# Sliding-window attention and MLP on one core: fill products on 64 rows, maxima of four heads at once, values by query block, division after the values

## Chip, cores and metric

The kernel runs on one core of a Trainium2 chip. The metric is the device time of one execution in microseconds (us). Lines of the profile name engines: PE is TensorE's products, PEld its weight loads, DVE is VectorE, ACT is ScalarE, POOL is GpSimd, SP is the queue that issues all DMA transfers of this kernel.

## What is computed

```python
def _A_ref(x, wqkv, wo):                    # x [1, 2048, 512], 32 heads of 16, window 256
    q, k, v = split_of(x @ wqkv)
    scores = einsum("bhqd,bhkd->bhqk", q, k) * 16 ** -0.5
    mask = (i - j >= 0) & (i - j < 256)
    p = softmax(where(mask, scores, -1e9))
    return einsum("bhqk,bhkd->bhqd", p, v).reshape(B, S, D) @ wo
def _B_ref(x, w1, b1, w2, b2):              # 1792 features
    return gelu(layernorm(x) @ w1 + b1) @ w2 + b2
xn = layernorm(x)
out = x + _A_ref(xn) * silu(_B_ref(xn))
```

## The kernel before

**Precision.** A product in full precision is three products of operands cut into a high and a low part (`PASSES`, L70: high·high, high·low, low·high). `split` (L72) makes the parts: a cast on ScalarE for the high one, a subtraction on VectorE for the low one.

**Operands.** The normalised x is kept transposed in `big` (high and low, 4 contraction tiles of 128, 2048 tokens). The 32 heads are worked on in 8 quads n of four heads. `job_qk` (L235) makes the query and key rows of quad n for a chunk c of 512 tokens: 12 products of 128 rows by 512 columns into one bank of PSUM, tile `pj`; its `finish` copies the bank to `pjr` (ScalarE), casts to `sh` (`high`, L257) and subtracts to `sl` (`low`, L264, GpSimd), and six DMAs (`send`, L248; four of `sh`, two of `sl`) lay the rows out in `slots[n % 2]`, tile `qk`. There a head has a strip of rows holding the high and low parts with which one 64-row product gives the scores in full precision; four rows hold the (negated) row maxima for the exponential. Each head of a pair p has its own half, rows 0 to 63 or 64 to 127, so the two products of a pair use different halves of TensorE. Tiles `sh` and `sl` are in pool `sgp`, which has one buffer of each.

**Slots.** The loop at L591 runs over slots t from -16 to 128. Slot t holds block t of the *probabilities* (quad t // 16, key block t % 16) and, `LEAD` = 12 blocks ahead, block m = t + 12 of the *maxima*. The order of one slot is written out:

```python
prob_block(t, pair 1); max_block(m, pair 0); fill_in(t, 0)
max_block(m, pair 1); prob_block(t, pair 0); fill_in(t, 1)
pv_step(t - 1); max_rows(m) if m % 4 == 3; plan[t]; out_rows
```

`Ordered` (L32) issues every instruction, so all lines of the profile are L42; it keeps the order of the program on every engine but SP, whose order a scheduler sets.

- `max_block` (L303): two score products of up to 384 keys into a two-bank tile `mx` (two such buffers), one predicated copy that writes the first key block over the masked part of the last one, and one reduction of 512 elements to two heads' maxima `mt`.
- `max_rows` (L323): negates the maxima of four blocks, cuts them into two parts, transposes them, and lays them out in the `qk` rows through a DRAM tile `mT_d`, by two DMAs.
- `prob_block` (L340): two score products, transposed, with 384 queries into a bank each (`st`, two buffers), an exponential of each on ScalarE (for the last 12 slots one exponential of both banks, into the free `mx` banks), and two maskings on GpSimd (`affine_select`). Result `pt`, 7 buffers.
- `pv_step` (L395): for key block kb, four heads' products into `otb`, one bank that collects 512 queries; the 17th value column is one, so the sum of the probabilities comes out beside the values. Every fourth block `out_chunk` (L378) transposes `otb` (VectorE), takes the reciprocal of the sums and multiplies (GpSimd), and `out_rows` (L389) transposes back and stores to `oT_d`.
- *Fills* are TensorE's other work, put between the products of a slot: in slots -16 to -1 quad 0's operands, all values of the first 16 heads (`job_v`, L273) and the transposes of x (`job_x`); from then on `job_qk` of quads 1 to 7, `job_v` of the other 16 heads (slots 49 to 77), and from slot 106 the transposes of y (`job_y`) and the first MLP products of six feature tiles (`job_h`, L464), which are kept in DRAM until the MLP. `level` (L533) spreads a job's products over its slots such that each slot holds TensorE about as long. `later` (L227) puts `high` one half slot and `low` three half slots behind a job's last product; the jobs of the four chunks of a quad follow each other at about four slots.
- `plan` holds other steps by slot: loading and splitting weights, the layernorm of y.

**MLP.** The loop over four chunks c at the end makes `hidden(f)` (12 products of 128x512 into `h`), `activate` (gelu, cast, subtraction) and `project` (12 products into four banks `acc`) for 14 feature tiles, software-pipelined by two; at f = 10 to 13 `load_o` (L642) loads and splits the attention values of 128 tokens each. At the end of a chunk come the products with `wo` (`s`, 12 of 512 columns for each block of 128 tokens), the gate, and the store.

Of the kernel before, what the change touches and what calls it, by code (L numbers as in the profile page):

```python
# [31 lines left out]
class Ordered:  # L32
    """an engine whose instructions keep the order of the program."""
# [16 lines left out]
def mixer_kernel(ctx, tc, x, wqk, wv, wo, w1, b1, w2, b2, out):  # L50
    """x [S,D]; wqk [NQ,128,KT*128]; wv [2,128,KT*256]; wo [128,4*512];
    w1 [128,NF*KT*128]; b1 [128,NF]; w2 [128,NF*512]; b2 [512]; out [S,D]."""
# [7 lines left out]
    ps_mx = ctx.enter_context(tc.tile_pool(name="ps_mx", bufs=2, space=PSUM))  # L60
    ps_st = ctx.enter_context(tc.tile_pool(name="ps_st", bufs=2, space=PSUM))
    ps_ot = ctx.enter_context(tc.tile_pool(name="ps_ot", bufs=1, space=PSUM))
    ps_pj = ctx.enter_context(tc.tile_pool(name="ps_pj", bufs=1, space=PSUM))
    attn = ExitStack()
    vp = attn.enter_context(tc.tile_pool(name="vp", bufs=1))
    pp = attn.enter_context(tc.tile_pool(name="pp", bufs=7))
    o2p = attn.enter_context(tc.tile_pool(name="o2p", bufs=1))
# [68 lines left out]
    XE, XO = ((pp, "pt"),), tuple((o2p, f"o2_{i}") for i in range(4))  # L136
    XA = (XE, XO, XE[:1] * 3 + ((t2, "t2"),), XO)

# [1 line left out]
    xs = {0: load_x(0, XA[0], "x")}  # L140
    big = bigp.tile([P, 2, KT, S], F32R, tag="big", name="xnT")       # x normalised, transposed; hi, lo
    x3 = bigp.tile([P, 4, 512], F32, tag="qk1", name="x_3")
    slots = []                                          # row, q/k, pair, token
# [7 lines left out]
    xn_d = dram.tile([4, P, D], F32, name="xn_d")      # the first chunk normalised  # L151
    oT_d = dram.tile([4, P, S], F32, name="oT_d")
    h_d = dram.tile([EARLY, P, 512], F32, name="h_d")          # the mlp's first products made early
    mT_d = dram.tile([NQ, NCH, 32, P], F32, name="mT_d")       # minus the row maxima, by rows
    otb = ps_ot.tile([P, 512], F32, name="otb")
# [13 lines left out]
    mask = upper.bitcast(I32).unsqueeze(1).to_broadcast([P, 2, P])  # L169
    neg = negc.unsqueeze(2).to_broadcast([P, 2, P])  # L170
    b1s = const.tile([P, NF], F32, name="b1s")

# [1 line left out]
    def job_x(c):  # L174
        box = []

        def mm(k):
            kt, i = k // 4, k % 4
            if i == 0:
                if kt == 2:  # L180
                    box.append(otb)
                elif kt == 3 and c == 0:
                    box.append(ps_mx.tile([P, 2, 512], F32, tag="mx", name="tr_0_3")[:, 0])
                else:
                    box.append((ps_st if kt < 2 else ps_pj).tile([P, 512], F32, tag="b", name=f"tr_{c}_{kt}"))
# [16 lines left out]
    def halves(dst_hi, dst_lo, src, part):  # L202
        """split in two steps, on ScalarE and on VectorE; part None: both."""
# [23 lines left out]
    def later(k, fn):  # L227
        """fn at k half slots from now."""
# [6 lines left out]
    def job_qk(n, c):  # L235
        """query and key rows of quad n, chunk c."""
# [4 lines left out]
        def mm(i):  # L241
            if i == 0:
                box.append(ps_pj.tile([P, 512], F32, tag="b", name=f"pj_{n}_{c}"))
# [29 lines left out]
    def job_v(hf, i):  # L273
        """value rows of token blocks 2i and 2i+1, 16 heads."""
        box = []

        def mm(k):
            if k == 0:
                box.append((ps_pj if hf else ps_st).tile([P, 2, 256], F32, tag="b", name=f"pv_{hf}_{i}"))
# [8 lines left out]

    def spread(jobs, places):
        """the jobs' products over the places, in order, each job in places of its own."""  # L290
# [10 lines left out]
    mts = {}  # L301

    def max_block(n, qb, p):  # L303
        slot = slots[n % 2]
        if qb % 4 == 0 and p == 0:
            mts[n, qb // 4] = small.tile([P, 2, 2, 4], F32, tag="mt", name=f"mt_{n}_{qb}")
        ps = ps_mx.tile([P, 2, 512], F32, tag="mx", name=f"mx_{n}_{qb}_{p}")
        lo = max(qb - 2, 0)
        off = 384 - P * (qb + 1 - lo)
        for a in range(2):  # L310
            r = slice(64 * a, 64 * a + 64)
            nc.tensor.matmul(ps[:, a, off:384], slot[r, 0, p, P * qb: P * (qb + 1)],
                             slot[r, 1, p, P * lo: P * (qb + 1)], start=True, stop=True)
        if qb < 2:
            nc.vector.copy_predicated(ps[:, :, 256:384], mask, neg)
            off = 256 - P * qb
        else:
            nc.vector.copy_predicated(ps[:, :, 256:384], mask, ps[:, :, 0:128])
            off = 128
        nc.vector.tensor_reduce(out=mts[n, qb // 4][:, :, p, qb % 4],  # L320
                                in_=ps[:, :, off:384], axis=AX.X, op=ALU.max)

    def max_rows(n, c):  # L323
        """minus the maxima, in two parts, as rows of the queries' operand."""
        mt = mts.pop((n, c))
        mh = small.tile([P, 2, 2, 2, 4], F32R, tag="mh", name=f"mh_{n}_{c}")     # head, part, pair, block
        nc.vector.tensor_scalar(mh[:, :, 0], mt, -1.0, None, op0=ALU.mult)
        nc.vector.scalar_tensor_tensor(mh[:, :, 1], mt, -1.0, mh[:, :, 0].bitcast(F32),
                                       op0=ALU.mult, op1=ALU.subtract)
# [8 lines left out]
    pts = {}  # L338

    def prob_block(n, kb, p):  # L340
# [3 lines left out]
        wide = 16 * n + kb + LEAD >= 16 * NQ       # no maxima are left: their banks are free  # L344
        if wide:
            both = ps_mx.tile([P, 2, 512], F32, tag="mx", name=f"st_{n}_{kb}_{p}")
        for a in range(2):
            r = slice(64 * a, 64 * a + 64)
            ps = both[:, a] if wide else ps_st.tile([P, 512], F32, tag="b", name=f"st_{n}_{kb}_{p}_{a}")
            nc.tensor.matmul(ps[:, 0:w], slot[r, 1, p, P * kb: P * (kb + 1)],  # L350
                             slot[r, 0, p, P * kb: P * kb + w], start=True, stop=True)
            if not wide:
                nc.scalar.activation(pt[:, a, 0:w], ps[:, 0:w], AF.Exp, scale=DH ** -0.5)
        if wide:
            nc.scalar.activation(pt[:, :, 0:w], both[:, :, 0:w], AF.Exp, scale=DH ** -0.5)
# [9 lines left out]
    def pv(n, c, kb, first, last):  # L365
        """what key block kb adds to query chunk c."""
        q0 = max(P * kb, 512 * c)
        q1 = min(P * kb + 384, 512 * (c + 1))
        for j in range(4):
            h = (4 * n + j) % 16  # L370
            nc.tensor.matmul(otb[32 * j: 32 * j + DH + 1, q0 - 512 * c: q1 - 512 * c], vt[:, kb, h],
                             pts[(n, kb, j // 2)][:, j % 2, q0 - P * kb: q1 - P * kb],
                             start=first, stop=last, skip_group_check=True,
                             tile_position=(0, 32 * j))

    o2 = {}

    def out_chunk(n, c):  # L378
        g, half = n // 2, n % 2
        T = t2.tile([P, 16, 32], F32, tag="t2", name=f"T_{n}_{c}")  # L380
        nc.vector.transpose(T.rearrange("p b r -> p (b r)"), otb)
# [384 lines left out]
```

## Time and profile before

| what | value |
|---|---|
| time, median of 3 runs (lowest to highest) | 826.49 us (825.32 to 826.92) |
| span of the profiled execution, first to last instruction | 826.1 us |
| mean clock granted to TensorE | 0.994 |
| DMA bytes | 70.77 MB, mean 86 GB/s |
| exponential of 128x384 / of 128x768, ScalarE | 489 ns (x408) / 814 ns (x20) |
| predicated copy of 128x256, VectorE | 421 ns (x224) |
| reduction of 128x512, VectorE | 693 ns (x240) |
| transposes of values `T` / `oT`, VectorE | 715 ns (x32) / 702 ns (x16) |
| copy `pjr` / cast `sh`, ScalarE | 587 ns / 621 ns (x32 each) |
| first slot with probabilities starts at / last maxima at | 76.5 us / 444.9 us |
| MLP from | 481.7 us |

The profile comes from one execution; what lies around its span shows in the table as the difference to the runs' times. "Busy" is the time in which an engine has an instruction under way. A group line gives line, engine, operation, tiles written and read, shapes, count, then busy time and mean duration, then the idle time ahead of the group and what ended it. The chain that ended last is followed back from the last instruction, at each step to what released it.

### The profile page before, as it was taken

The numbers are of one execution on the slowest core, as the hardware profiler recorded it, in microseconds if no ns is written. First come the engines' busy times: TensorE is split into PE (matmuls) and PEld (weight loads), VectorE is DVE, ScalarE is ACT, GpSimd is POOL, SyncE is SP. The second block draws the span as 40 slices with busy tenths as digits, with TensorE's granted clock in tenths as the row PEclk, the third lists the DMA queues.
The fourth block names the chain that finished last, engine by engine and source line by source line (L and its number), as shares of the span: only waits on it lengthen the run. The fifth ranks groups of instructions, "written<-read, shape, count | busy, mean of one in ns | idle before, by whom it ended". The sixth has DMA issues, their size and how long they took to land.

```text
span 826.1 us, 13927 instructions
## 1 busy us (share of the span) xinstructions
PE 804.7 (97%) x4864; PEld 533.2 (65%) x4864; DVE 528.2 (64%) x1073; ACT 367.3 (44%) x747; POOL 286.4 (35%) x591
## 2 busy tenths in 40 slices
PE   5899999999999999999999999999999999999997
PEld 4676444444455666444444468888888888888886
DVE  6696788998878667999996438652445245432233
ACT  5533666766656565566677752322112211221111
POOL 4001665666555445566677511020000100020002
PEclk9899999999999999999999999999999999999999
DMA  8534434343242432433343463430013100210021
GB/s 273 160 65 92 96 80 108 94 107 82 58 106 61 113 66 46 120 92 78 87 105 107 140 217 102 127 115 13 14 47 90 56 13 24 66 52 1 25 64 63
DMA packets 53332, 70.77 MB, mean 86 GB/s; under 512 B 10192, under 2 KB 22480, under 8 KB 53264
## 3 DMA queue, kind: packets, MB, share of 16 engines
q1 hardware_dynamic: 53264, 69.89, 31.5%
q8 instruction: 39, 0.64, 0.3%
q14 instruction: 29, 0.24, 0.1%
HBM read 30.68 MB, written 11.53 MB: 51 GB/s over the span
## 4 chain that ended last, share of the span: by engine, by line
PE 92%; DVE 3%; ACT 2%; DMA 1%; issue 1%; POOL 0%; SPq 0%; POOLq 0%; ACTq 0%; DVEq 0%
PE h L42 19%; PE acc L42 19%; PE pj L42 15%; PE otb L42 11%; PE st L42 10%; PE mx L42 8%; PE pv L42 6%; PE s L42 5%; DMA x<-in_x_dram 1%; DVE xnT L42 1%; DVE mt L42 1%; PE yt L42 1%; ACT x L42 1%; ACT pjr L42 0%; DVE bnA L42 0%
## 5 line engine op out<-in xcount | busy, mean ns | idle before, releaser
L42 ACT ACTIVATE pt<-st 128x384 f32<-128x384 f32 (+2 forms) x488 | 211.8, 484 | 137.1 <-PE st L42 108.3
L42 POOL TENSOR_SCALAR_AFFINE_SELECT pt<-pt 128x256 f32<-128x256 f32 x480 | 187.2, 413 | 203.6 <-ACT pt L42 201.7
L42 DVE TENSOR_REDUCE mt<-mx 128x2 f32<-128x512 f32 (+1 forms) x256 | 173.1, 676 | 8.8
L42 PE MATMUL h<-yh,w1s 128*128 128x512 f32 x448 | 150.5, 396 | 0.0
L42 PE MATMUL pj<-xnT,wqb 128*128 128x512 f32 x384 | 140.6, 452 | 0.1
L42 PE MATMUL acc<-w,gh 128*128 128x512 f32 x448 | 139.5, 393 | 0.0
L42 DVE COPY_PREDICATED mx<-upper,mx 128x256 f32<-128x256 int32 x224 | 94.2, 421 | 39.1 <-PE mx L42 36.3
L42 DVE CAST gh<-g 128x512 fp32r<-128x512 f32 x56 | 23.9, 426 | 144.0 <-PE acc L42 124.6
L42 ACT ACTIVATE g<-h,b1s 128x512 f32<-128x512 f32 x50 | 34.4, 689 | 181.4 <-PE h L42 180.6
L42 PE MATMUL st<-qk 64*128 64x384 f32 (+2 forms) x512 | 112.0, 393 | 1.3 <-ACT pt L42 1.3
L42 PEld LDWEIGHTS st<-qk 64*128 64x128 f32 x512 | 59.4, 184 | 73.5 <-ACT pt L42 58.1
L42 PE MATMUL mx<-qk 64*128 64x384 f32 (+2 forms) x512 | 100.3, 387 | 4.0 <-DMA qk<-sl 2.6
L42 PE MATMUL otb<-pt,vt 128*17 128x384 f32 (+2 forms) x1408 | 102.4, 388 | 0.0
L42 PEld LDWEIGHTS h<-yh,w1s 128*128 128x128 f32 x448 | 83.6, 188 | 21.2 <-issue 3.9
L42 PEld LDWEIGHTS acc<-w,gh 128*128 128x128 f32 x448 | 84.2, 188 | 17.9
L42 PEld LDWEIGHTS pj<-xnT,wqb 128*128 128x128 f32 x384 | 64.4, 192 | 41.1 <-issue 28.8
L42 POOL TENSOR_TENSOR xo<-xo,gated 128x512 f32<-128x512 f32 x16 | 20.6, 1287 | 195.8 <-DVE gated L42 188.6
L42 PE MATMUL h<-w1s 128*128 128x512 f32 x224 | 87.9, 393 | 0.0
L42 PE MATMUL acc<-w,gl 128*128 128x512 f32 x224 | 87.2, 389 | 0.0
L42 PEld LDWEIGHTS mx<-qk 64*128 64x128 f32 x512 | 49.2, 185 | 44.8 <-issue 37.4
L42 PE MATMUL pv<-wva,xnT 128*128 128x256 f32 x384 | 54.8, 291 | 0.6
L42 PEld LDWEIGHTS otb<-pt,vt 128*17 128x17 f32 x1408 | 28.0, 96 | 40.9 <-issue 17.8
(79 smaller groups left out, 731.1 us busy)
## 6 DMA issues: line engine op xcount, KB each, us to landing
qk<-sh SPq DMA_DIRECT2D x128, 128.0 KB
qk<-sl SPq DMA_DIRECT2D x64, 128.0 KB
x<-in_x_dram SPq DMA_DIRECT2D x16, 256.0 KB
oT_d<-oT SPq DMA_DIRECT2D x16, 256.0 KB
or<-oT_d SPq DMA_DIRECT2D x16, 256.0 KB
xo<-in_x_dram SPq DMA_DIRECT2D x16, 256.0 KB
out_dram<-xo SPq DMA_DIRECT2D x16, 256.0 KB
w1r<-in_w_dram SPq DMA_DIRECT2D x14, 256.0 KB
```

Source lines behind the costliest of these rows:

```text
L42: r = issue(*args, **kwargs)
```

## The change

**PSUM.** The pools are replaced by fixed tiles: `xy` (2 banks, maxima: the last 256 keys of four heads), `zo` (2 banks: the first 128 keys of four heads, and `otb` in a quarter of the second bank), `stb` (2 banks, one pair of transposed scores), `fb` (2 single banks for fills). Pool `pp` has 8 buffers instead of 7, pool `o2p` goes.

**Fills.** `pair_qk`, `pair_v` and `pair_h` take the place of `job_qk` (from quad 1), `job_v` (last 16 heads) and `job_h`. In `pair_qk`, `finish` (called with t = t1, the last slot) plans `high` and `low` by slot. `tandem` runs two jobs together in two phases: in each unit one product is on rows 64 to 127 of one job and one on rows 0 to 63 of the other, into different banks; the second phase takes the other halves.

```diff
+    def tandem(t0, t1, one, two, mid=None, back=None):
+        n = one[0]
+        lo, hi = slice(0, 64), slice(64, P)
+        mid = mid or max(1, (t0 + t1 + 1) // 2)
+        first = [(t, k) for t in range(t0, mid) for k in range(2)]
+        second = [(t, k) for t in range(back or mid, t1) for k in range(2)] + [(t1, 0)]
+        for phase, places in enumerate((first, second)):
+            for i in range(n):
+                flags = dict(start=(phase == 0 and i == 0), stop=(phase == 1 and i == n - 1), skip_group_check=True)
+                def unit(i=i, phase=phase, flags=flags):
+                    (two if phase == 0 else one)[1](fb[1 - phase], i, hi, **flags)
+                    (one if phase == 0 else two)[1](fb[phase], i, lo, **flags)
+                fills.setdefault(places[i * len(places) // n], []).append((unit, ()))
+        fills[t1, 0].append((one[2], (fb[0], t1)))
+        fills[t1, 0].append((two[2], (fb[1], t1)))
...
+            at(t + 1 + c % 2, high)
+            at(t + 1 + c % 2, low)
...
-        level(t0, n, [job_qk(1, c)])
...
+    for n, spans in enumerate((((-2, 2), (3, 8)), ((9, 15), (16, 23)), ((24, 31), (32, 39)), ((40, 46), (47, 51)),
+                               ((56, 59), (68, 71)), ((76, 79), (80, 85)), ((86, 91), (92, 97))), 1):
+        for c, (t0, t1) in zip((0, 2), spans):
+            tandem(t0, t1, pair_qk(n, c), pair_qk(n, c + 1))
+    for i, (t0, t1) in enumerate(((52, 55), (60, 63), (64, 67), (72, 75))):
+        tandem(t0, t1, pair_v(2 * i), pair_v(2 * i + 1))
+    for f, *at_ in ((2, 106, 112, None, None), (4, 113, 119, 115, None), (6, 120, 127, 123, 125)):
+        tandem(*at_[:2], pair_h(f), pair_h(f + 1), *at_[2:])
```

**Maxima.** One `max_block` a slot for four heads: eight products of 128 or 256 keys, one predicated copy, one reduction with negation, so `max_rows` copies and subtracts only.

```diff
+        for p, a, first in ((0, 1, True), (0, 0, False), (1, 1, True), (1, 0, False),
+                            (0, 1, False), (1, 1, False), (0, 0, True), (1, 0, True)):
+            if qb >= 2 or not first:
+                scores(p, a, first)
+        four = xy.rearrange("q a (p k) -> q a p k", p=2)
+        nc.vector.copy_predicated(four[:, :, :, 128:256], mask,
+                                  neg if qb < 2 else zo[:, :, 0:256].rearrange("q a (p k) -> q a p k", p=2))
+        nc.vector.tensor_reduce(out=mts[n, qb // 4][:, :, :, qb % 4],
+                                in_=four[:, :, :, off:256], axis=AX.X, op=ALU.max, negate=True)
```

**Probabilities.** `prob_block` writes the pair into `stb` (for pair 1 of the last 12 slots into `xy`) and always takes one exponential of both banks.

**Values.** `pv_step` goes by query block: for each of up to three key blocks, four products of 128 queries into `otb`; VectorE copies `otb` to an SBUF tile `oraw`, and every fourth block a DMA stores the undivided values and their sums to `oT_d` (now 8 x 32 rows a pair of quads). `out_chunk` and `out_rows` go.

**Order of a slot.** The maxima stand in one place, and `plan` stands ahead of the last scores:

```diff
         if 0 <= t < end:
             prob_block(t // 16, t % 16, 1)
-        if 0 <= m < end:
-            max_block(m // 16, m % 16, 0)
         fill_in(t, 0)
         if 0 <= m < end:
-            max_block(m // 16, m % 16, 1)
+            max_block(m // 16, m % 16)
+        fill_in(t, 1)
+        for fn, args in plan.get(t, []):
+            fn(*args)
         if 0 <= t < end:
             prob_block(t // 16, t % 16, 0)
-        fill_in(t, 1)
         if t >= 1:
             pv_step((t - 1) // 16, (t - 1) % 16)
```

**Division.** In the MLP's first chunk `fetch_sums` loads the sums (f = 1), VectorE takes one reciprocal of 128x512 (f = 4), and it is stored to `rden_d`. `load_o(c, g)` loads 128 rows of values by 512 tokens and the reciprocals spread over the rows; `split_o`, one f later, multiplies on GpSimd and splits. Some slots of weight loading, splitting and layernorm steps in `plan` are moved too.

More of the change, by code (lines that the diff above doesn't have):

```diff
@@ L134, in load_x @@
                 for i in range(4)]
-    XE, XO = ((pp, "pt"),), tuple((o2p, f"o2_{i}") for i in range(4))
-    XA = (XE, XO, XE[:1] * 3 + ((t2, "t2"),), XO)
-    xs = {0: load_x(0, XA[0], "x")}
+    XE = ((pp, "pt"),)
+    xs = {0: load_x(0, XE, "x")}
     big = bigp.tile([P, 2, KT, S], F32R, tag="big", name="xnT")
-    x3 = bigp.tile([P, 4, 512], F32, tag="qk1", name="x_3")
+    x23 = bigp.tile([P, 8, 512], F32, tag="qk1", name="x_23")
     slots = []
@@ L151, in mixer_kernel, with bank @@
     xn_d = dram.tile([4, P, D], F32, name="xn_d")
-    oT_d = dram.tile([4, P, S], F32, name="oT_d")
+    oT_d = dram.tile([4, 8, 32, S], F32, name="oT_d")
+    rden_d = dram.tile([4, 8, S], F32, name="rden_d")
     h_d = dram.tile([EARLY, P, 512], F32, name="h_d")
     mT_d = dram.tile([NQ, NCH, 32, P], F32, name="mT_d")
-    otb = ps_ot.tile([P, 512], F32, name="otb")
+    xy = psum.tile([P, 2, 512], F32, name="xy")
+    zo = psum.tile([P, 2, 512], F32, name="zo")
+    otb = zo[:, 1, 256:384]
+    stb = psum.tile([P, 2, 512], F32, name="stb")
+    fb = [psum.tile([P, 512], F32, name=f"fb{i}") for i in range(2)]
+    turn = {"st": 0, "fb": 0}
+    def bank(kind="st"):
+        turn[kind] ^= 1
+        return stb[:, turn[kind]] if kind == "st" else fb[turn[kind]]
     vt = vp.tile([P, NKB, 16, DH + 1], F32, name="vt")
@@ L179, in mm @@
             if i == 0:
[L180 to L185, printed above, removed]
+                box.append(bank() if kt < 2 else zo[:, 1] if kt == 2 else xy[:, 0] if c == 0 else bank("fb"))
             nc.tensor.transpose(box[kt][:, P * i: P * (i + 1)], xs[c][i][:, P * kt: P * (kt + 1)], ident)
@@ L287, in job_v, with pair_qk, mm, send @@
         return [(109, mm, k) for k in range(24)], finish
+    def pair_qk(n, c):
+        ops = [(kt, a, b) for kt in range(KT) for a, b in PASSES]
+        sl = slice(512 * c, 512 * (c + 1))
+        def mm(ps, i, r, **flags):
+            kt, a, b = ops[i]
+            nc.tensor.matmul(ps, wqs[n][r, a, kt], big[r, b, kt, sl], **flags)
+        def send(src, qk, tt):
+            copy_rows(slots[n % 2][tt:P:4, qk, :, sl], src[64 * qk: 64 * qk + 64])
+        def finish(ps, t):
+            hi = sgp.tile([P, 512], F32R, tag="sh", name=f"sh_{n}_{c}")
+            lo = sgp.tile([P, 512], F32R, tag="sl", name=f"sl_{n}_{c}")
+            raw = t2.tile([P, 512], F32, tag="t2", name=f"pjr_{n}_{c}")
+            nc.scalar.copy(raw, ps)
+            def high():
+                nc.scalar.copy(hi, raw)
+                if n >= 2:
+                    copy_rows(slots[n % 2][3:P:32, 0, :, sl], slots[n % 2][7:P:32, 0, :, sl])
+                for qk, tt in ((1, 0), (0, 0), (1, 2), (0, 1)):
+                    send(hi, qk, tt)
+            def low():
+                nc.gpsimd.tensor_tensor(lo, raw, hi.bitcast(F32), op=ALU.subtract)
+                send(lo, 1, 1)
+                send(lo, 0, 2)
+            at(t + 1 + c % 2, high)
+            at(t + 1 + c % 2, low)
+        return 3 * KT, mm, finish
@@ new lines, in pair_v, with mm, finish, pair_h @@
+    def pair_v(i):
+        def mm(ps, k, r, **flags):
+            j, kt, (a, b) = k // 12, k % 12 // 3, PASSES[k % 3]
+            kb = 2 * i + j
+            nc.tensor.matmul(ps[:, 256 * j: 256 * (j + 1)], big[r, a, kt, P * kb: P * (kb + 1)], wva[r, b, kt],
+                             **flags)
+        def finish(ps, t):
+            nc.scalar.copy(vt[:, 2 * i: 2 * i + 2, :, 0:DH], ps.rearrange("p (b h d) -> p b h d", b=2, d=DH))
+        return 6 * KT, mm, finish
+    def pair_h(f):
+        def mm(ps, k, r, **flags):
+            kt, (a, b) = k // 3, PASSES[k % 3]
+            nc.tensor.matmul(ps, mlp["w1"][r, a, f, P * kt: P * (kt + 1)], mlp["yy"][b][kt][r], **flags)
+        def finish(ps, t):
+            raw = t2.tile([P, 512], F32, tag="t2", name=f"hr_{f}")
+            nc.scalar.copy(raw, ps)
+            nc.sync.dma_start(h_d[f - 2], raw)
+        return 3 * KT, mm, finish
@@ L301, in mixer_kernel, with max_block, scores @@
     mts = {}
-    def max_block(n, qb, p):
+    def max_block(n, qb):
         slot = slots[n % 2]
-        if qb % 4 == 0 and p == 0:
+        if qb % 4 == 0:
             mts[n, qb // 4] = small.tile([P, 2, 2, 4], F32, tag="mt", name=f"mt_{n}_{qb}")
[L307 to L310, printed above, removed]
+        lo = max(qb - 1, 0)
+        off = 128 * (lo + 1 - qb)
+        def scores(p, a, first):
             r = slice(64 * a, 64 * a + 64)
[L312 to L321, printed above, removed]
+            out, keys = ((zo[:, a, P * p: P * (p + 1)], slice(P * (qb - 2), P * (qb - 1))) if first else
+                         (xy[:, a, 256 * p + off: 256 * (p + 1)], slice(P * lo, P * (qb + 1))))
+            nc.tensor.matmul(out, slot[r, 0, p, P * qb: P * (qb + 1)], slot[r, 1, p, keys], start=True, stop=True)
+        for p, a, first in ((0, 1, True), (0, 0, False), (1, 1, True), (1, 0, False),
[6 more added lines that the diff above has]
+        nc.vector.tensor_reduce(out=mts[n, qb // 4][:, :, :, qb % 4],
+                                in_=four[:, :, :, off:256],
+                                axis=AX.X, op=ALU.max, negate=True)
     def max_rows(n, c):
@@ L343, in prob_block @@
         pt = pp.tile([P, 2, 384], F32, tag="pt", name=f"pt_{n}_{kb}_{p}")
[L344 to L347, printed above, removed]
+        both = xy if p and 16 * n + kb + LEAD >= 16 * NQ else stb
+        for a in (1, 0):
             r = slice(64 * a, 64 * a + 64)
-            ps = both[:, a] if wide else ps_st.tile([P, 512], F32, tag="b", name=f"st_{n}_{kb}_{p}_{a}")
-            nc.tensor.matmul(ps[:, 0:w], slot[r, 1, p, P * kb: P * (kb + 1)],
+            nc.tensor.matmul(both[:, a, 0:w], slot[r, 1, p, P * kb: P * (kb + 1)],
                              slot[r, 0, p, P * kb: P * kb + w], start=True, stop=True)
[L352 to L355, printed above, removed]
+        nc.scalar.activation(pt[:, :, 0:w], both[:, :, 0:w], AF.Exp, scale=DH ** -0.5)
         nc.gpsimd.affine_select(out=pt[:, :, 0:P], in_=pt[:, :, 0:P], pattern=[[0, 2], [1, P]],
@@ L362, in prob_block @@
         pts[(n, kb, p)] = pt
[L365 to L381, printed above, removed]
-        rec = small.tile([P, 16], F32, tag="rec", name=f"rec_{n}_{c}")
-        nc.vector.reciprocal(rec.unsqueeze(2), T[:, :, DH: DH + 1])
-        if half == 0:
-            o2[c] = o2p.tile([P, 16, 2, DH], F32, tag=f"o2_{c}", name=f"o2_{g}_{c}")
-        later(1, lambda: nc.gpsimd.tensor_tensor(o2[c][:, :, half], T[:, :, 0:DH],
-                                rec.unsqueeze(2).to_broadcast([P, 16, DH]), op=ALU.mult))
@@ L389, in out_rows @@
[L389 to L403 removed]
+    outs = {}
@@ new lines, in pv_step @@
+    def pv_step(n, qb):
+        lo = max(qb - 2, 0)
+        for kb in range(lo, qb + 1):
+            for j in range(4):
+                nc.tensor.matmul(otb[32 * j: 32 * j + DH + 1], vt[:, kb, (4 * n + j) % 16],
+                                 pts[n, kb, j // 2][:, j % 2, P * (qb - kb): P * (qb - kb + 1)],
+                                 start=(kb == lo), stop=(kb == qb),
+                                 skip_group_check=True, tile_position=(0, 32 * j))
+        if qb % 4 == 0:
+            outs[0] = sgp.tile([P, 512], F32, tag="or", name=f"oraw_{n}_{qb}", bufs=2)
+        nc.vector.tensor_copy(outs[0][:, P * (qb % 4): P * (qb % 4 + 1)], otb)
+        if qb % 4 == 3:
+            nc.sync.dma_start(oT_d[n // 2, n % 2::2, :, P * (qb - 3): P * (qb + 1)], outs[0])
@@ L448, in y_transpose @@
         if ps is None:
-            ps = otb if kt % 2 else ps_pj.tile([P, 512], F32, tag="b", name=f"yt_{c}_{kt}")
+            ps = zo[:, 1] if kt % 2 else fb[1]
         for i in range(4):
@@ L460, in mm @@
         def mm(i):
[L461 removed]
+            y_transpose(0, kt, fb[kt % 2])
         return [(436, mm, 0)], lambda: None
[L464 to L477 removed]
     plan = {}
@@ L486, in mixer_kernel @@
     fetch_wv(0)
-    xs[1] = load_x(1, XA[1], "x")
-    xs[2] = load_x(2, XA[2], "x")
-    xs[3] = [x3[:, i] for i in range(4)]
+    xs[1] = load_x(1, XE, "x")
+    for c in (2, 3):
+        xs[c] = [x23[:, 4 * (c - 2) + i] for i in range(4)]
+    for i in range(4):
+        nc.sync.dma_start(xs[2][i], x[1024 + P * i: 1024 + P * (i + 1), :])
     nc.gpsimd.memset(mhalf, -0.5)
@@ L578, in mixer_kernel @@
         (_, mm, _), = job_y(kt)[0]
-        fills[106 + kt, 1] = [(mm, (0,))]
-    level(110, 18, [job_h(f) for f in range(2, EARLY + 2)])
+        fills[101 + kt, 1] = [(mm, (0,))]
     ln3 = layernorm(xs[3], "A3", True)
@@ L649, in mixer_kernel @@
     for c in range(NCH):
-        accs = [ps_mx.tile([P, 2, 512], F32, tag="mx", name=f"acc_{c}_{i}") for i in range(2)]
+        accs = [xy[:, 0], xy[:, 1], zo[:, 0], fb[0]]
         gs, os_, hs = {}, [], {}
@@ L704, in mixer_kernel @@
                     y_steps(5, 10)
+            if c == 0 and f == 1:
+                den = fetch_sums()
+            if c == 0 and f == 4:
+                nc.vector.reciprocal(den, den)
+                nc.sync.dma_start(rden_d.rearrange("g a (c t) -> (g a c) t", c=NCH), den)
+            if 11 <= f < 15:
+                os_.append(split_o(c, f - 11, *wanted))
             if 10 <= f < 14:
-                os_.append(load_o(c, f - 10))
-        us = [accs[i // 2][:, i % 2] for i in range(4)]
+                wanted = load_o(c, f - 10)
+        us = [accs[i] for i in range(4)]
         for u in us:
```

115 lines of the change are left out of this document (34 added, 81 removed).

## Prediction

> **What bounds the kernel now.** I read, in this order: the engine table and the chain that ended last (both on the page), the busy time by stage, the groups by shape, and the timelines of TensorE, its weight loads, ScalarE and SP between 200 and 212 us.
>
> ```profile
> PE 804.7 (97%) x4864; PEld 533.2 (65%) x4864; DVE 528.2 (64%) x1073; ACT 367.3 (44%) x747; POOL 286.4 (35%) x591
> PE 92%; DVE 3%; ACT 2%; DMA 1%; issue 1%; POOL 0%; SPq 0%; POOLq 0%; ACTq 0%; DVEq 0%
> ```
>
> TensorE is busy for 97% and is 92% of the chain. By stage (columns: us, then busy us and instructions of PE, PEld, DVE, ACT, POOL, then clock, DMA share, GB/s):
>
> ```profile
> 28.50:76.50 48.00, 47.65 (x272) 35.52 (x272) 34.76 (x70) 14.59 (x25) 0.65 (x1) 0.94 0.35 75
> 76.50:444.90 368.40, 365.34 (x2729) 187.39 (x2728) 310.03 (x641) 236.43 (x547) 227.60 (x498) 1.00 0.37 88
> 444.90:481.80 36.90, 36.90 (x265) 17.41 (x261) 13.75 (x24) 26.39 (x42) 20.18 (x50) 1.00 0.38 123
> 481.80:826.00 344.20, 339.31 (x1513) 279.61 (x1512) 149.71 (x284) 71.73 (x107) 27.73 (x23) 1.00 0.20 64
> ```
>
> These stages are slots -12 to -1, slots 0 to 115 (scores, maxima, values, fills), slots 116 to 128 (no maxima left) and the MLP. In the second, 3.18 us a slot, VectorE is at 84%: the next bound is close.
>
> ```profile
> 206.21 0.44 PE L42 MATMUL st<-qk 64*128 64x384 f32 x2
> 206.49 0.34 PE L42 MATMUL mx<-qk 64*128 64x384 f32 x2
> 206.76 0.73 PE L42 MATMUL pj<-xnT,wqb 128*128 128x512 f32 x2
> 207.42 0.44 PE L42 MATMUL mx<-qk 64*128 64x384 f32 x2
> ```
> ```profile
> 206.21 0.19 PEld L42 LDWEIGHTS st<-qk 64*128 64x128 f32 x2 [0.64 <-ACT pt L42]
> 206.31 0.19 PEld L42 LDWEIGHTS mx<-qk 64*128 64x128 f32 x2
> ```
>
> Two 64-row products of a pair start together (2 to 11 ns apart instruction by instruction); the pair streams in 168 ns, and the next pair's weights are loaded 104 ns after its own, while it still streams. Entering or leaving the 128-row fills exposes one load (107 ns) and one drain (92): a maxima pair alone between fills takes 0.367 us of the chain.
>
> **What the change costs, part by part.**
>
> *TensorE.* Two jobs' 64-row halves side by side stream as long as one 128-row job each (512 columns: 226 ns a product in both), so the fills keep their time, and about two switches a slot go. Values take 12 products of 128 columns (101 to 109 ns for four heads) instead of the 128/256/384 mix: the same. TensorE alone would gain.
>
> *One score buffer.* The pair in `stb` must be read before the next is written. From st0's first product: 0.335 for 384 columns, 0.044 to the exponential's start, 0.814 for it (the 128x768 form, x20, of the last slots), 0.052 to the next weight load, 0.107 for that: 1.35 us. The next pair adds 0.17, the eight small maxima products 0.5. **Loop P is 2.05 us plus the fill**; values hide under the exponential (0.82).
>
> *Maxima of four heads, loop M.* One buffer `xy`, so everything is in series. Eight products of 128 or 256 columns, bound by their loads of 115 to 126 ns: 4 x 0.126 = 0.50 to the last one, 0.217 for that, 0.044 to VectorE. The predicated copy of 512 elements: 256 took 421 ns, a reduction of 256 took 426 and of 512 693, so 1.04 ns an element: 0.688 + 0.034 (dependent start). The reduction of 1024: 1.226 - 0.085 (an independent successor starts that much early). Then the copy of `otb` out of `zo`, which stands behind the reduction on VectorE and ahead of the next maxima: 0.29 (128 elements; 0.225 to 0.29). Then 0.052 and 0.107 for the next load. **Loop M is 3.05 us** (2.95 with the load at 115 and the short copy; 3.15 if each dependent step costs 30 ns more).
>
> So the second stage is VectorE's: 116 x 3.05 = 353.8. Other VectorE work now falls into this loop: weight splits 6 x 0.6 and 2 x 0.8, y statistics 4 x 0.77 and applications 4 x 0.48, yt 4 x 0.6, w1 4 x 0.67: 15.3. In 30 slots fills (0.9 to 1.8 us) make loop P longer by 14.2 together, the y transposes add 2.5, and the 14 first blocks of a quad save 6.7. Sum 379 against 368.4: **+10.6** (at 2.95 about 0; at 3.15 and P 2.13 +21.5). The transposes (715 ns x32, 702 x16) that go had been beside TensorE; that is already in loop M, which lacks them.
>
> *The sends' wait*, the decisive term. A pair's two jobs end at one place; `high` runs one slot later for the even chunk and two for the odd, and tile `sh` has one buffer. The odd chunk's cast on ScalarE, 3.05 us behind the even one's, therefore waits until all four sends of the even one have landed, and the exponential of st0 is queued behind it, then st1 (one score buffer), then the maxima.
>
> ```profile
> 201.28 0.62 ACT L42 CAST sh<-pjr 128x512 fp32r<-128x512 f32 x1
> ```
> ```profile
> 201.93 0.57 SPq L42 DMA_DIRECT2D qk<-sh  x1
> 202.60 0.53 SPq L42 DMA_DIRECT2D qk<-mT_d  x1
> 203.19 1.84 SPq L42 DMA_DIRECT2D qk<-sh  x3
> 206.71 1.17 SPq L42 DMA_DIRECT2D qk<-sl  x2
> ```
>
> SP takes 0.53 to 0.61 us an issue. The first send issued at 201.93 landed at 204.24 (2.3 later), the last, issued 204.43, between 206.8 and 208.2: 4.9 to 6.3 us after the cast's end. Before, casts are about four slots apart and the wait never appears. After: even cast ends 0.85 into its slot's maxima, the last send lands at 6.15 (5.05 to 7.4), the odd cast was due at 3.3. The exponential moves from 4.2 to 6.9, the next maxima from 6.15 to 8.5: **2.35 us a pair**. Bounds: 1.2 (no mT transfer between the sends) to 4. 14 pairs: 33, less 2.8 where other VectorE work of those slots hides in the wait, plus 2 in slot 4, where quad 1's first maxima need sends of slot 3: **+32** (17 to 56).
>
> *Last slots.* With no maxima and no switches the 13 slots are two exponentials (0.814 + 0.05 + 0.107) plus little: 25.6 instead of 36.9: **-11** (+-3). *Slots before 0*: two switches of 0.2 a slot less: **-2.5** (-4 to 0). *MLP and late division*: one reciprocal of 128x512 (0.5 to 3.4), on VectorE at 43%; 16 multiplications on GpSimd (1.287 each, the `xo` form) a tile after the load, GpSimd at 8% there; the `o` splits keep their size: **+1** (0 to 4; if the products `s` waited for them, 1.3 a chunk more). SP issues 32 loads instead of 16 in 344 us, and 32 stores of values instead of 16 in 368 us, at 0.6 each: on a queue that is mostly idle, hidden; a store that falls between two sends would add 0.6 to that wait, inside its bounds.
>
> Sum on the profiled execution's span: 826.1 + 10.6 + 32 - 11 - 2.5 + 1 = 856.2. The median of the runs is 0.4 above the span, less than a run's spread (825.32 to 826.92). **I predict 856 us.**
>
> **Rivals.**
> 1. *The wait has cover, and maxima keep pace: faster.* If sends land about 1 us sooner and the mT read lies elsewhere, the wait goes under loop M; with M at 2.95: 826 + 0 + 2 - 12.5 = about 815, down to 806 with M at 2.9. It decides at about 5.05 us from slot start to the last landing. For: the sends' first landing took 2.3 us. Against: four issues at 0.6 on one queue are 2.4 by themselves, and a straggler needed 3.7.
> 2. *64-row loads exposed between successive pairs.* Then a product pair of the fills takes 0.32 instead of 0.226, and the same sum of slots is 406: 883. Against: the load at 206.31 under the products of 206.21, in the same rows.
> 3. *Maxima products in series or halves not side by side.* Eight in series put 0.4 on both loops: 905. Halves in series double the fills: 935; that would be the change not doing what it says. Against: starts 2 to 11 ns apart. Both write other banks than their partner, as the pairs of the trace do.
>
> The Trainium skill (TensorE: Matmul & The Clock Gate, Part 3: Packing small matmuls, "What overlaps and what doesn't") says that a weight load overlaps running products only where the row groups differ. By it rival 2 would come true; the two loads shown, 104 ns apart in the same rows, speak against it in this kernel, so it keeps a small chance.
>
> **How the numbers follow.** Forecast (838 to 876) 0.62; rival 1 (806 to 832) 0.23, of which 0.03 lies within 0.2% (824.8 to 828.1, about what a measurement of this kernel can tell from no change) and 0.02 above; rival 2 (876 to 890) 0.08; rival 3 0.07. Faster 0.18, same 0.03, slower 0.79. The range 815 to 885 leaves out rival 3, half of rival 2 and about half of rival 1's faster part: 0.2.
>
> **What would show it.** ScalarE idle ahead of the cast `sh`, released by a DMA, 14 times by 2 to 3 us; VectorE's copies and reductions (0.69, 1.23) at a period of 3.05; TensorE idle ahead of `mx` and `st`, released by VectorE and ScalarE; slots 116 on at 2.0 us; fill pairs at 226 ns. Wrong it is if the odd cast runs on time, if reductions take under 1.15, or if fill pairs take over 0.3.

## The result, and the profile after

The changed kernel takes 954.55 us (median of 4 runs, 952.88 to 957.29), the kernel before 826.1 us beside it. The ratio is 1.156, 95% interval 1.153 to 1.159: slower, as forecast, but 98.5 us above the 856 that I gave and outside the range. The profiled execution has a span of 954.3 us.

The engine table of the page of the changed kernel, and its row of granted clock in 40 slices:

```profile
PE 800.4 (84%) x7384; PEld 615.7 (65%) x7384; DVE 491.7 (52%) x866; ACT 349.8 (37%) x515; POOL 289.1 (30%) x575
PEclk9889989989999999888799999889999999899999
```

TensorE is busy about as long as before (800 to 805 us) and idle for 154 us instead of 21. Its mean granted clock fell from 0.994 to 0.939. By stage (columns as in the prediction's table; the bounds are starts of the maxima's reductions in slots -12, 0 and 115, and the end of the last exponential):

```profile
33.30:87.50 54.20, 46.60 (x324) 39.06 (x322) 32.30 (x47) 16.03 (x27) 0.78 (x2) 0.87 0.29 65
87.50:512.10 424.60, 350.11 (x4994) 255.90 (x4994) 270.67 (x457) 220.11 (x317) 212.56 (x467) 0.92 0.35 91
512.10:538.90 26.80, 25.55 (x434) 17.27 (x438) 11.14 (x25) 23.64 (x38) 17.25 (x45) 1.00 0.37 112
538.90:954.30 415.40, 358.88 (x1536) 287.53 (x1528) 156.64 (x283) 71.77 (x107) 47.60 (x39) 0.96 0.19 64
```

With the same bounds in the trace before, and those of the experiments that follow:

| us | to slot -12 | slots -12 to -1 | 0 to 114 | 115 on | MLP |
|---|---|---|---|---|---|
| before | 29.5 | 48.1 | 365.6 | 37.4 | 345.5 |
| changed | 33.3 | 54.1 | 424.6 | 26.8 | 415.5 |
| e1: one-bank tiles in the MLP | 33.5 | 54.0 | 421.0 | 26.8 | 363.8 |
| e2: odd cast later | 34.2 | 53.3 | 379.6 | 26.8 | 420.5 |
| e3: both, and the start | 30.7 | 43.1 | 380.8 | 26.8 | 364.9 |
| e4: e3, fills on 128 rows | 30.6 | 43.4 | 435.8 | 29.4 | 364.3 |
| e5: e3, no division | 30.2 | 43.4 | 379.8 | 26.8 | 346.4 |
| e6: e3, division in own tiles | 30.3 | 43.1 | 380.7 | 26.8 | 350.2 |
| e7: e3, late fills, copy on ScalarE | 31.0 | 42.7 | 376.3 | 27.7 | 364.4 |
| e8: e6 and e7 | 30.6 | 42.7 | 376.3 | 28.9 | 352.1 |
| e9: e6, weights' low parts on GpSimd | 31.8 | 43.1 | 377.5 | 26.9 | 349.4 |
| e10: e8 and e9, some fills in both halves | 31.1 | 45.0 | 367.2 | 28.4 | 353.8 |
| e11: e10, quad 1 sooner | 30.5 | 45.0 | 366.1 | 27.5 | 352.4 |

Against before, slots 0 to 114 lose 59 us, the MLP 70 and the start 10, and the last slots give 11 back.

A plain slot, VectorE's timeline of the changed kernel (start, duration, instruction, idle time ahead and what ended it):

```profile
194.40 0.70 DVE L42 COPY_PREDICATED xy<-upper,zo 128x512 f32<-128x512 int32 x1 [0.83 <-PE zo L42]
195.13 1.23 DVE L42 TENSOR_REDUCE mt<-xy 128x4 f32<-128x1024 f32 x1
196.28 0.28 DVE L42 COPY oraw<-zo 128x128 f32<-128x128 f32 x1
197.39 0.69 DVE L42 COPY_PREDICATED xy<-upper,zo 128x512 f32<-128x512 int32 x1 [0.83 <-PE zo L42]
```

From one predicated copy to the next it is 2.99 us: 0.70, 1.23 and 0.28 of work, and 0.83 in which VectorE waits for the eight products. This is loop M.

A slot with the sends' wait, ScalarE, then SP, then TensorE:

```profile
203.18 0.61 ACT L42 CAST sh<-pjr 128x512 fp32r<-128x512 f32 x1
...
209.49 0.62 ACT L42 CAST sh<-pjr 128x512 fp32r<-128x512 f32 x1 [3.24 <-DMA qk<-sh]
```
```profile
204.04 1.20 SPq L42 DMA_DIRECT2D qk<-sh  x2
205.29 0.55 SPq L42 DMA_DIRECT2D qk<-mT_d  x1
205.89 1.71 SPq L42 DMA_DIRECT2D qk<-sh  x2
```
```profile
207.19 0.41 PE L42 MATMUL zo<-pt,vt 128*17 128x128 f32 x8 [0.45 <-POOL pt L42]
210.87 0.69 PE L42 MATMUL stb<-qk 64*128 64x384 f32 x2 [3.26 <-ACT pt L42]
211.35 1.06 PE L42 MATMUL fb<-xnT,wqb 64*128 64x512 f32 x4
```

ScalarE stands still for 3.24 us ahead of the odd chunk's cast; TensorE, two steps behind it, for 3.26. The waits name `sh` behind the DMA 14 times, 38.2 us in all. What follows on TensorE is slow as well, and the busy time of the four stretches (columns as above) says why:

```profile
207.60:210.80 3.20, 0.01 (x1) 0.00 (x0) 0.91 (x2) 1.31 (x2) 0.00 (x1) 0.78 0.78 172
210.80:214.90 4.10, 3.97 (x34) 2.84 (x34) 1.55 (x2) 1.64 (x3) 2.72 (x5) 0.50 0.59 154
```

The granted clock falls to 0.50 inside the idle stretch and is still 0.50 in the 4.1 us after it; the trace's record of the clock has it there until 216.2 us. Fill pairs there start 0.42 us apart instead of 0.23.

In the MLP, TensorE's starts with an idle time ahead, around the end of the second chunk:

```profile
725.18 1.12 PE L42 MATMUL zo<-ident,y 128*128 128x128 f32 x4 [4.80 <-DVE zo L42]
...
732.83 0.66 PE L42 MATMUL zo<-ident,y 128*128 128x128 f32 x4 [2.37 <-ACT gated L42]
...
740.89 3.03 PE L42 MATMUL stb<-wos,ohl 128*128 128x512 f32 x12 [0.78 <-DVE gated L42]
744.77 0.50 PE L42 MATMUL stb<-yh,w1s 128*128 128x512 f32 x1 [0.85 <-DVE gated L42]
...
752.63 0.50 PE L42 MATMUL stb<-yh,w1s 128*128 128x512 f32 x1 [2.12 <-ACT g L42]
```

The longest waits are at `zo`. Its first bank is one of the four accumulators, its second takes transposes of the next chunk's y. These transposes start only when VectorE has added the bias to the accumulator (4.80 us) or ScalarE has read it for the gate (2.37 us). In the same way products into one bank of `stb` start only when an engine has read the *other* bank: `s` of block i + 1 behind the gate of block i, the second `h` behind the gelu of the first. Over the whole MLP TensorE stands still for 24.7 us at `zo` (6 times) and for 16.6 us at `stb` (15 times). The program holds these waits: it treats the two banks of one tile as one.

### The profile page after: what moved, and what is told of

Read it like the earlier page. It is cut to its first block, busy times and chain, and to the rows that moved or that the text cites. A ratio compares the mean times of both kernels' runs of the same rounds, so it can differ in the third digit from the quotient of the medians.

```text
span 954.3 us, 18265 instructions
## 1 busy us (share of the span) xinstructions
PE 800.4 (84%) x7384; PEld 615.7 (65%) x7384; DVE 491.7 (52%) x866; ACT 349.8 (37%) x515; POOL 289.1 (30%) x575
## 5 line engine op out<-in xcount | busy, mean ns | idle before, releaser
L42 ACT ACTIVATE pt<-stb 128x768 f32<-128x768 f32 (+1 forms) x244 | 189.0, 775 | 163.4 <-PE stb L42 153.8
L42 DVE TENSOR_REDUCE mt<-xy 128x4 f32<-128x1024 f32 (+1 forms) x128 | 152.6, 1192 | 4.4
L42 DVE COPY_PREDICATED xy<-upper,zo 128x512 f32<-128x512 int32 x112 | 78.0, 696 | 141.5 <-PE zo L42 136.8
L42 PE MATMUL stb<-yh,w1s 128*128 128x512 f32 x400 | 132.6, 394 | 7.6 <-ACT g L42 5.0
L42 PE MATMUL stb<-qk 64*128 64x384 f32 (+1 forms) x488 | 101.7, 409 | 42.0 <-ACT pt L42 38.9
L42 PE MATMUL zo<-pt,vt 128*17 128x128 f32 x2880 | 109.2, 285 | 23.8 <-DVE xy L42 21.2
L42 PE MATMUL fb<-xnT,wqb 64*128 64x512 f32 (+1 forms) x720 | 129.1, 425 | 0.0
L42 DVE CAST gh<-g 128x512 fp32r<-128x512 f32 x56 | 26.9, 480 | 165.1 <-ACT g L42 155.6
L42 PE MATMUL xy<-qk 64*128 64x256 f32 (+2 forms) x536 | 90.6, 320 | 3.9 <-DMA qk<-sl 3.5
L42 PEld LDWEIGHTS stb<-yh,w1s 128*128 128x128 f32 x400 | 75.9, 190 | 26.2 <-ACT g L42 6.3
L42 PE MATMUL stb<-w1s 128*128 128x512 f32 x200 | 78.6, 393 | 0.0
```

Source lines behind the costliest of these rows:

```text
L42: r = issue(*args, **kwargs)
```

## The experiments

**e1: the MLP with one-bank tiles.** My theory for the 70 us: `xy`, `zo` and `stb` are tiles of two banks, and a wait for one bank holds the other up too. The rival: the late division, or the lower clock.

```diff
+    attn_banks.close()
+    ps_c = ctx.enter_context(tc.tile_pool(name="ps_c", bufs=1, space=PSUM))
+    one = lambda name: ps_c.tile([P, 512], F32, name=name)
+    acc4, hb, mlp["yt"] = [one(f"acc{i}") for i in range(4)], [one(f"hb{i}") for i in range(2)], [one(f"ytb{i}") for i in range(2)]
...
-        accs = [xy[:, 0], xy[:, 1], zo[:, 0], fb[0]]
+        accs = acc4
```

> The MLP alone gets PSUM tiles of one bank each (four for acc, two for h and s, two for the transposes of y) instead of the two-bank tiles xy, zo and stb; the late division stays. Theory (a wait for one bank of a two-bank tile holds up the other bank as well): the stretch from the last exponential to the end falls from 415 us to about 350, the time from 954.5 to about 890. Rival (the late division, its loads and multiplications, or the lower granted clock makes the MLP long): the stretch stays above 400 us and the time above 940.

Measured: 902.22 us (ratio to before 1.091, interval 1.090 to 1.093), the MLP 363.8. 52 of the 70 us are the shared tiles; 18 are not, so the theory is right for the larger part only.

**e2: the odd chunk's cast later.**

```diff
-            at(t + 1 + c % 2, high)
-            at(t + 1 + c % 2, low)
+            at(t + 1 + 3 * (c % 2), high)
+            at(t + 1 + 3 * (c % 2), low)
```

> The odd chunk's cast into sh comes three slots behind the even one's instead of one (t1 + 4 instead of t1 + 2), nothing else. Theory (14 waits for the one buffer sh): the 14 slots of 6 to 7.5 us become about 3.0 and their successors lose 0.7, in all 45 to 55 us: about 902. As the prediction sized it (2.35 a pair): 33 us less, about 921. Rival (the wait only uncovers another one, for instance of the maxima on the same rows): above 940.

Measured: 915.95 us (ratio 1.107, 1.103 to 1.111). Slots 0 to 114 fall by 45.0, from 424.6 to 379.6: slots 17, 33 and 41 (6.80, 6.97, 6.25 us) are 2.98 each. No wait is left at `sh` behind a DMA. The time fell by 38.6 only and is nearer to 921 than to 902: the MLP of the profiled execution was 5.0 us longer (420.5), and why it was, no run shows.

One wait also shows what the half clock adds. In slot 61 of the changed kernel ScalarE waits 3.00 us for the sends, the clock stays whole, and slots 61 and 62 take 2.3 us more than in e2. In e1, whose slots have the same instructions, the wait is 3.07 us, the clock falls, and the two slots take 3.9 us more. Slot 61 of the changed kernel, then of e1 (columns as above):

```profile
309.20:315.10 5.90, 3.45 (x68) 3.13 (x68) 2.12 (x3) 1.93 (x3) 2.38 (x4) 1.00 0.47 95
308.60:315.90 7.30, 4.78 (x67) 4.50 (x67) 2.09 (x4) 1.92 (x3) 2.35 (x4) 0.77 0.58 141
```

**e3: e1 and e2, and one-bank tiles for the fills before slot 0.**

> e1 and e2 together, and also one-bank tiles for the fills of the slots before 0 (stb is opened at slot 0 in their place). Theory: 65 + 50 + 10 us less than the changed kernel, about 830, within 1.5% of the kernel before; slots 0 to 115 at VectorE's 2.98 us where the fill is under 0.9. Rival (the parts overlap, one wait hides another): above 850.

Measured: 849.86 us (ratio 1.027, 1.026 to 1.029). The start with slots -12 to -1 falls from 87.4 to 73.8 us, below the 77.6 of before. The parts add up; what was expected of the MLP (350) and so of the whole (830) was 15 to 20 too low.

**e4: fills on 128 rows.** e3 with the fills as before in form, so that what the pairs of 64 rows bring can be read.

```diff
-                    (two if phase == 0 else one)[1](fb[1 - phase], i, hi, **flags)
-                    (one if phase == 0 else two)[1](fb[phase], i, lo, **flags)
+                    (two if phase else one)[1](fb[phase], i, slice(0, P), **flags)
```

> e3 with the fills of slots 0 on as 128-row products, one job after the other in the same places (as many steps as there were pairs). If pairs of 64 rows save the two changes of tiling mode a slot (0.2 us each), the slots with a fill over 0.6 us get up to 0.4 us longer: 10 to 25 us slower than e3. If pairs bring nothing beside a bound of 2.98 on VectorE: within 5 us of e3.

Measured: 905.12 us (ratio 1.095, 1.091 to 1.099), 55 us slower than e3. Slots 0 to 114 are 55.0 us longer, the last slots 2.6. TensorE in a slot of e4:

```profile
201.76 0.44 PE L42 MATMUL stb<-qk 64*128 64x384 f32 x2 [0.27 <-ACT pt L42]
202.13 0.73 PE L42 MATMUL fb<-xnT,wqb 128*128 128x512 f32 x2
202.79 0.32 PE L42 MATMUL zo<-qk 64*128 64x128 f32 x1
...
203.45 0.50 PE L42 MATMUL fb<-xnT,wqb 128*128 128x512 f32 x1
203.88 0.44 PE L42 MATMUL stb<-qk 64*128 64x384 f32 x2
```

The score pair from 201.76 holds TensorE for 0.37 us until the fill starts; in e3 such a pair ahead of a fill holds it for 0.28 (medians of the slots, here and below). The two products from 202.13 hold it for 0.66 us, two pairs side by side in e3 for 0.47; the eight maxima products from 202.79 for 0.66, in e3 for 0.44; the one product from 203.45 for 0.43, a pair in e3 for 0.28. That is 0.65 us in a slot with two fills, or 0.33 for entering and leaving one. Slots with two products in each half take 3.70 us (median) in e4 and 2.99 in e3. I had expected 10 to 25; VectorE's loop does not hide the switches. The loop that e7 takes up would explain that, since the fill ahead of the maxima lies in it.

**e5 and e6: the late division.** What was left of the MLP, 19 us, lies in the first chunk. VectorE of e3:

```profile
502.38 3.35 DVE L42 RECIPROCAL den<-den 128x512 f32<-128x512 f32 x1
...
561.57 0.43 DVE L42 CAST ohl<-or 128x512 fp32r<-128x512 f32 x1 [5.56 <-POOL or L42]
```

The reciprocal stands ahead of the next cast of `gh`, and the values of the last quads come late. e5 leaves the division out; e6 keeps it, without buffers of `t2` for the loads and with the reciprocal in four pieces:

```diff
-        raw = load(t2, "t2", oT_d[g, :, 0:DH, cols], f"or_{c}_{g}")
-        rec = load(t2, "t2", bass.AP(...), f"rec_{c}_{g}")
+        ohl = gp.tile([P, 2, 512], F32R, tag="ohl", name=f"ohl_{c}_{g}", bufs=4)
+        nc.sync.dma_start(ohl[:, 0].bitcast(F32), oT_d[g, :, 0:DH, cols])
+        nc.sync.dma_start(ohl[:, 1].bitcast(F32), bass.AP(...))
...
-            if c == 0 and f == 4:
-                nc.vector.reciprocal(den, den)
+            if c == 0 and 4 <= f < 8:
+                nc.vector.reciprocal(den[:, 128 * (f - 4): 128 * (f - 3)], den[:, 128 * (f - 4): 128 * (f - 3)])
```

> e3 without the late division: the sums are not fetched, no reciprocal is taken or loaded, and the values go undivided into the product with wo, so the output is not the reference's. Theory (what is left of the MLP's loss, 364.9 us after 345.5, is the late division, in the first chunk: the reciprocal of 3.35 us on VectorE, and the loads of rec that wait for buffers of t2): the stretch from the last exponential to the end falls to 347 to 352, the time to about 835. Rival (TensorE's restarts or the MLP's own loads at its start make it): above 360.

> e3 with the late division, but values and reciprocals loaded into the two halves of the ohl tile that later holds their parts (no t2 buffer is needed to load), and the reciprocal in four pieces of 128x128 over f = 4 to 7. Theory (t2's five buffers hold the loads up): about 8 to 12 us less than e3, 838 to 842. Rival (the transfers or GpSimd's multiplications themselves): within 3 us of e3.

Measured: e5 830.33 us (ratio 1.004, 1.003 to 1.006), MLP 346.4; e6 833.12 us (1.009, 1.007 to 1.010), MLP 350.2. Without the division the MLP is as before (345.5), so the rest of the 70 us is the division, 18.5 us; 14.7 of them are the buffers and the one long reciprocal, not GpSimd's multiplications. How much each of these two is, no run tells apart.

**e7: fills behind the maxima, and the copy of `otb` on ScalarE.** In e3, slots with 0.68 us of fill ahead of the maxima and none behind take 3.2 us, though loop P would be 2.7. My theory is a third loop: the values' products wait for the predicated copy (they write `otb`, in a bank of `zo` that the copy reads), and the next scores, the fill and the maxima stand behind them on TensorE: 2.53 us plus the fill ahead of the maxima. The wait is in the traces (67 times in e3, 23.5 us); that it closes a loop of this length is what e7 tries.

```diff
-        first = [(t, k) for t in range(t0, mid) for k in range(2)]
-        second = [(t, k) for t in range(back or mid, t1) for k in range(2)] + [(t1, 0)]
+        first = [(t, 1) for t in range(t0, mid) for k in range(2)]
+        second = [(t, 1) for t in range(back or mid, t1) for k in range(2)] + [(t1, 0)]
...
-        nc.vector.tensor_copy(outs[0][:, P * (qb % 4): P * (qb % 4 + 1)], otb)
+        nc.scalar.copy(outs[0][:, P * (qb % 4): P * (qb % 4 + 1)], otb)
```

> e3 with all fills of slots 0 on in the second half of their slot (behind the maxima), and the copy of otb on ScalarE instead of VectorE. Theory of three loops (VectorE 2.98 us with the copy and 2.70 without it; values wait for the predicated copy because they share tile zo with the first keys' scores, 2.53 plus the fill ahead of the maxima; scores and exponentials 2.01 plus the slot's whole fill): slots of 2.70 where the fill is under 0.7, slots 0 to 115 about 20 us shorter than in e3 (381 to about 361), the time about 830. Rival (ScalarE's copy delays the exponentials, so the third loop grows by 0.28): no gain, 845 to 865.

> e6 and e7 together: 850 - 10 - 20 = about 820, below the kernel before. If the rival of e7 holds: about 840 to 850.

Measured: e7 844.03 us (ratio 1.022, 1.020 to 1.024), slots 0 to 114 at 376.3, 4.5 less than e3 and not 20; plain slots 2.82 us instead of 2.98 (2.70 expected). Slots 48 to 77, where the fills are large, got 3.5 us longer. e8, with e6 in it, is 830.77 us (1.006, 1.003 to 1.008), where I had expected 820. The gain is real and a quarter of the size; what takes the 0.12 us more in a plain slot I did not isolate, and no run takes the two parts of the edit apart.

**e9, e10, e11: a version that beats both.** e9 subtracts low parts of weights on GpSimd instead of VectorE. e10 joins e8 and e9, with the fills of slots 47 to 77 and of quad 1's first pair of chunks in both halves again. e11 casts quad 1 a slot sooner and has the fills of its second pair in both halves too (`heavy` marks such fills):

```diff
-            at(t + 1 + 3 * (c % 2), high)
-            at(t + 1 + 3 * (c % 2), low)
+            at(t + (n > 1) + 3 * (c % 2), high)
+            at(t + (n > 1) + 3 * (c % 2), low)
...
-        heavy = 46 < t0 < 78 or t0 < 0
+        heavy = 46 < t0 < 78 or t0 < 9
```

> e6 with the low parts of the weights wqk (quads 2 to 7), wv and w1 (four more tiles) subtracted on GpSimd instead of VectorE. Theory (VectorE sets slots 0 to 115, so each such subtraction in a slot lengthens it by 0.6 to 0.8 us): slots 6, 21, 22, 26, 37, 53, 73, 83, 111, 112, 114 go from 3.6 to about 3.0, in all 5 to 8 us: about 826. Rival (GpSimd's maskings stand behind a subtraction of 1.29 us and the values wait for them): no gain.

> e8 and e9 together, and the fills of slots 47 to 77 in both halves of a slot again (e8's stretch 48 to 78 was 3.5 us longer than e3's): 830.8 - 3.5 - 6.5 = about 821, below the kernel before (826.4). Rival as in e9: about 827.

> e10 with quad 1's casts one slot sooner (t1 and t1 + 3) and its fills in both halves of a slot. Theory: slots 3 and 4 (6.6 and 4.1 us in e10) wait only for the sends of quad 1's first chunk, so about 3 us go there, and 1 us in slot 7 (5.0): about 823, 0.3 to 0.5% below the kernel before. Rival (SP's queue is what is late in slots 2 to 4, with the stores of values and maxima ahead): no gain, 827.

Measured: e9 830.0 us (ratio 1.004, 1.002 to 1.005), slots 0 to 114 3.2 us shorter than e6, half of what I expected. e10 827.34 us (1.001, 0.999 to 1.002): as long as before, and not the 821 expected. e11 820.97 us (0.992, 0.990 to 0.995): 0.8% below the kernel before. Slots 3, 4 and 7 took 6.61, 4.06 and 5.02 us in e10 and take 4.05, 2.76 and 3.01; that is 5.9 us of the 6.4 between the two medians, with two edits that no run takes apart. In the profiled executions slots 0 to 114 are only 1.1 us shorter: in e11 TensorE's granted clock was 0.50 from 385.5 to 399.0 us (1.00 in e10), and slots 98 to 101, which lie almost wholly there, took 3.6 us more.

## Why the prediction was right and wrong

- **The bound of slots 0 on** was right. Copy 0.696, reduction 1.226, `otb` copy 0.282 us against 0.688, 1.226 and 0.29; a period of 2.98 against 3.05. (The terms as listed add up to 3.08 for loop M and 2.02 for loop P, not 3.05 and 2.05.) With the wait taken away the slots sum to 379.6 in e2, against 379 forecast (for one slot more). The sum is closer than its terms: loop M was 0.07 us too long a slot (VectorE's wait for the eight products is 0.83 us, and the terms give 0.92); the wait of the values for the predicated copy through `zo` was missing, for the prediction had only the half that makes the maxima wait for the `otb` copy; and slots 3 and 4 take 10.5 us in e2, 4.6 above two plain slots, where the sends' term had 2. "Values hide under the exponential" does not hold where the values wait for that copy.
- **The sends' wait** was the right mechanism, with ScalarE, SP and 14 pairs as told, and too small: 45.0 us in e2 (32 forecast, 56 the upper bound). The wait itself was sized well: the last of the four sends lands at 209.35 us, 5.6 after the even cast's end at 203.79, between the 4.9 and 6.3 read from before, and the one full wait at whole clock (slot 61) cost 2.3 us against 2.35 forecast. What I left out is what follows it: TensorE idles for 3 us and then works at a granted clock of 0.50 for some 5 us, so the wait's own slot and the next get longer; slot 34 behind the wait shown takes 0.7 us more than in e2. Not all 14 were like this: in slot 4 the wait cost nothing and in slot 48 0.6 us.
- **Slots before 0** were wrong in sign: +9.8 us (start included) instead of -2.5. The switches go, but `stb` as one tile makes the next bank's product wait for the copy out of the other; with one-bank tiles e3 gives -3.8.
- **Last slots**: -10.6 us, -11 forecast.
- **MLP**, the step that failed: "+1 (0 to 4...)". I priced the division's instructions and took all else as unchanged, though the change also takes the MLP's banks from the fixed tiles: the waits between two banks of one tile were put at nothing, without a reason. Measured +70: 52 from these tiles (e1), 18.5 from the division (e5), 14.7 of which are the loads' buffers and the reciprocal's place on VectorE (e6). The prediction weighed GpSimd and SP and no buffer.
- **Rivals.** Rivals 2 and 3 fell: fill pairs start 0.23 us apart at full clock, as do 128-row products, and from the first to the last start of the eight maxima products it is 0.40 to 0.45 us (202.65 to 203.05 in one slot). Rival 1 needed the wait to have cover; it had none; and with the wait, the tiles and most of the division's cost gone (e6) the kernel is still 0.9% slower than before, at VectorE's 2.98.

The 128 us in sum: 45 the wait, 14 the slower loops, 70 the MLP, 10 the start, and 11 back from the last slots. Of the 98 us above the forecast 69 are the MLP, 13 the sends' wait, 12 the start with the slots before 0, and the rest the slower loops.

## What to carry to other kernels

When PSUM pools are replaced by fixed tiles, walk through every stage that uses them, also those that the change is not about: two banks in one tile wait as one. When two jobs are made to end together, look at every one-buffer tile behind them; their spacing was what hid its transfers. And count a stall of TensorE of 2 to 3 us at more than its length where the clock falls in it: in slot 61 the same wait cost 2.3 us without and 3.9 with the fall.

## What the runs showed of the chip

- Around an idle stretch of 3.2 us TensorE was granted half its clock (0.50, fill pairs 0.42 us apart instead of 0.23), for 5.4 us after it. The Trainium skill (TensorE: Matmul & The Clock Gate, Part 1: The HAM clock gate) says that the clock falls to half after an idle window of about 3.4 us and comes back after as long a busy one. This trace agrees in the half and in a step of 3.41 us, of which every stretch at half clock inside the changed kernel's span is a multiple (3.41 to 13.65). It does not agree in the idle window: the fall came 1.8 us after TensorE's last product, and behind stalls of 2.2 us as well.
- It went with the share of work in a step instead. From 20 us to 4 us before its end, the changed kernel's clock fell 22 times, each time at the end of a step of 3.41 us. In 20 of these steps TensorE was busy for 1.51 us or less, in the other two for 1.75 and 2.24. In all steps at full clock that no fall followed it was busy for 1.53 us or more.
- The mean granted clock follows the idle time: 0.939 in the changed kernel, 0.949 in e1, 0.958 in e2, 0.979 in e3, 0.988 in e6, 0.994 before. It rises as the waits go, so it follows from them, and what it adds (slot 61) is part of their price.
- In the bank of `zo` that holds `otb`, TensorE's values and VectorE's read of the first keys' scores take turns. By the Trainium skill (PSUM — Partial Sum Buffer, PSUM bank collisions raise a hardware error) that is a rule of the chip: two engines may not use one bank on the same partitions at once. No run here tries it. The waits between the two banks of one tile in the MLP are no such rule: e1 and e3 have one-bank tiles there, and are faster.
